# One-input steps of ranking and lists through PSUM, and a second last routing batch whose weights move behind the token splits, in a fused attention and expert kernel

## The chip, the cores and the metric

The kernel runs on one core of a Trainium2 chip. The metric is device time in microseconds (us) of one launch, as the median of three runs. A profile of one further execution gives the times of single instructions; all times in this document count from the start of that execution's span.

Engines are called by the names in the profile: PE (TensorE, matrix products), PEld (its weight loads), DVE (VectorE), ACT (ScalarE), POOL (GpSimd) and SP (SyncE, which issues DMAs). Each engine works through its own queue in order. SBUF is the memory that all engines share; PSUM holds the results of PE in banks of 128 x 512 fp32, and DVE and ACT can read and write it too.

## The reference

Causal attention with a decay bias over 8 batches, 8 heads, 576 positions and 64 columns a head; its output, 4608 tokens of 512 columns, is routed to one of 16 experts each (4 groups of 4), and each token's result is its expert's, scaled by two softmax weights:

```python
x = attn_out.transpose(0, 2, 1, 3).reshape(4608, 512)
g_logits = x @ w_group;  g_idx = np.argmax(g_logits, axis=1)
for g in range(4):
    xg = x[g_idx == g]
    e_logits = xg @ w_expert[g];  e_idx = np.argmax(e_logits, axis=1)
    for e in range(4):
        h = np.maximum(xg[e_idx == e] @ w1[g, e], 0.0)      # 512 -> 1024
        out[tokens] = (g_w * e_w)[:, None] * (h @ w2[g, e])  # 1024 -> 512
```

All data are fp32. The kernel gets the precision of an fp32 product from three products of rounded parts: high by high, low by high and high by low.

## The kernel before, in words

**Attention** handles 64 heads in 32 pairs, p = 0 to 31; a batch b is four pairs. For each head PE makes row maxima (`pm`), scores (`ps`) and the product with the values (`po`); the pair's output is normalised on DVE (`xT`, L352), split in a high part (`xTh`, on ACT) and a low part (`xTl`), turned on PE (`px`, L394) and written to `xs` in device memory. The order of this stage is written out by hand in strings of letters; `R` in them takes one step of the **router** (class `Router`), a generator for each batch.

**Routing a batch** (`Router.batch`): PE makes the logits (`lg`, `pl`, `pr`), turns them so that tokens lie on partitions (`plt`, L795); DVE finds the best group and expert of each token (L803 to L824, which ends with the one-hot `hot`); PE counts how many tokens each expert has (`pc`, L831); DVE gives each token a place in its expert's list (L848 to L873), and fills `val` with the parts of the token's number (L879). PE adds them to the lists (`listed(0, 2)`: `pi`, L886). `weights` makes the token's combined weight in three bf16 parts, L940 puts them in `val`, and `listed(2, 5)` (`pw`, L886) adds them to the lists as well.

**The transition** overlaps the last two routed batches (b = 6 and 7) with the start of the experts. `pick(0)`, run by the generator `first()` ahead of batch 6, chooses the first expert from the counts so far; `start()` in batch 6 lists its first 256 tokens, gathers their rows (`xg`, an indirect DMA on POOL's queue), and then runs `pick(1)` for the second expert, whose number `e` SP reads to load its weights (`raw`, L1015). The first expert is slot 0 with 256 tokens (class `Slot`: transposes `px` and splits `xh`, `xl` at L1069 to L1072, hidden layer `ph` L1131, output `py` L1186); the third group of 128 tokens of this expert comes from a list that is complete only after batch 7 (class `Tile`: `prr_x`, `xhr`, `xlr`, then products `pur`, L1273). Here the order of PE is the order of the code, and the other engines are put in order by a scheduler, with constraints: `after(...)` keeps what it encloses behind the instructions given, and `behind(tc, later, earlier)` keeps one instruction behind another.

**The weights of every expert** come as fp32 (`raw`) and are split in a high part on ACT (`wh`, L1017) and a low part on POOL (`wl`, L1020), or, for some pieces, on DVE (L1026, from a copy `pw` in PSUM).

**After batch 7** DVE takes the lists of all experts apart and ranks the experts by token count: `list_ids` (L617 to L619) makes token numbers of list entries and marks the empty ones, `order_key` and L1331 to L1337 rank the experts, `by_slot` (L1355) picks each slot's list. On DVE `xlr`, for which PE waits, comes behind most of these steps. Slots 1 to 15 then run one expert each, in the order of the ranks; this stage has an order of its own for PE, DVE and ACT, which the change leaves as it is.

Of the kernel before, what the change touches and what calls it, by code (L numbers as in the profile page):

```python
# [20 lines left out]
P = 128  # L21
# [3 lines left out]
E = 16  # L25
# [29 lines left out]
def attn_moe(ctx, tc, qk, v, s, wr, w1, w2, out, stop_at=None, dbg=None):  # L55
# [24 lines left out]
    st.listed = {}  # L80
    st.masks, st.av, st.gathered, st.lows = [], [], [], []
# [30 lines left out]
def attention(tc, qk, v, s, wr, xs, st):  # L112
# [3 lines left out]
    with ExitStack() as ctx:  # L116
# [138 lines left out]
        def scores(n, pt):  # L255
# [16 lines left out]
            def exps(u, ps, o):  # L272
                t, off, w = u[0]
                rows = KT[t][1]
                nc.scalar.activation(probs(pt, t, off)[:rows, 0:o], ps[:rows, :o], AF.Exp, scale=0.125)  # L275
                if u[0][1] == 0:
                    push("e", n, lambda: causal(u))
# [46 lines left out]
        def normalise(p, vals, sums):  # L324
# [31 lines left out]
            def high():  # L356
# [8 lines left out]
                st.xh = nc.scalar.copy(xh, x[:, 0:512])  # L365
                push("L", p, lambda: low(xh, xl, x))
# [16 lines left out]
        def route(b):  # L383
            if b == B - 2:
                rt[0].queue.append(rt[0].first())
            rt[0].queue.append(rt[0].batch(b, xtail.pop(b), *xhl.pop(b)))
# [235 lines left out]
def first_ids(nc, pool, st, c0, c1, want):  # L622

    V = nc.vector
    sh = [P, c1 - c0, E]
# [11 lines left out]
class Router:  # L637
# [72 lines left out]
    def logits(self, b, xh, xl, chunks):  # L710
# [9 lines left out]
        if chunks[-1] == 3:  # L720
            self.logged = b
            nc.tensor.matmul(ps[:52], self.wr_sb[:, 3], xh[:, 3], start=False, stop=True)
            return self.lg.pop(b)

    def pick(self, k):
# [6 lines left out]
        top = sm.tile([P, 1], F32, name=f"ktop{k}")  # L732
        V.tensor_reduce(out=top, in_=st.key, axis=AX.X, op=ALU.max)
        V.tensor_tensor(out=st.first[:, k], in0=st.key, in1=top.to_broadcast([P, E]), op=ALU.is_equal)
        t = sm.tile([P, E], F32, name=f"kt{k}")
# [8 lines left out]
    def start(self):  # L744

        nc, sm, st = self.tc.nc, self.sm, self.st
        V = nc.vector
        chosen = first_ids(nc, sm, st, 0, 2, ((0, 0, 2, st.ids0[:, 0:2]),))
# [5 lines left out]
        with after(self.tc, chosen):  # L754
            self.pick(1)
            t = sm.tile([P, E], F32, name="ku")
            V.tensor_scalar(out=t, in0=st.count, scalar1=-1.0, scalar2=256.0, op0=ALU.mult, op1=ALU.add)
            V.scalar_tensor_tensor(out=t, in0=t, scalar=0.0, in1=st.first[:, 0], op0=ALU.max, op1=ALU.mult)
            V.tensor_tensor(out=st.count, in0=st.count, in1=t, op=ALU.add)
        yield  # L760

    def batch(self, b, xtail, xh, xl):
# [9 lines left out]
        lT = self.lT  # L772

# [15 lines left out]
        nc.scalar.copy(xr, ps[:64, :])  # L789
        st.xrt = (nc.scalar if b == B - 1 else nc.sync).dma_start(self.xs[b * S + 512:(b + 1) * S], xr)  # L790
# [3 lines left out]
        for t in range(NB):  # L794
            nc.tensor.transpose(ps[:, t * 20:(t + 1) * 20], lT[:, t * P:(t + 1) * P], ident[:20, :20])  # L795
# [81 lines left out]
        C4 = [P, NB, E * NL]  # L877
        for j in range(2):
            (nc.gpsimd if b < B - 1 else V).tensor_tensor(  # L879
                out=val[:, j], in0=colf, in1=self.part[:, j, b].unsqueeze(2).to_broadcast(C4), op=ALU.mult)  # L880
# [14 lines left out]
        def weights(bank):  # L895
            nc.scalar.activation(ex, df, AF.Exp)
            yield 1
# [4 lines left out]
            V.tensor_reduce(out=wf, in_=ex, axis=AX.X, op=ALU.add)  # L902
# [18 lines left out]

        yield 2
        if b == B - 1:
            c3, c3p = yield from weights(self.ps_s(f"pk{b}"))
        pi = listed(0, 2, "pi")
        if b == B - 1:
            st.routed = first_ids(nc, sm, st, 0, 3, ((0, 2, 3, st.ids0[:, 2:3]), (1, 0, 3, st.ids1)))
        else:
            if b == B - 2:
                for _ in self.start():  # L930
                    yield
            c3, c3p = yield from weights(pi)
        for j in range(3):
            yield
            with after(tc, st.routed):
                if b < B - 1 and j == 0:
                    nc.gpsimd.tensor_tensor(out=val[:, 2 + j], in0=colf, in1=c3[:, j].unsqueeze(2).to_broadcast(C4),
                                            op=ALU.mult)
                else:
                    st.valued = V.tensor_tensor(out=val[:, 2 + j], in0=colf,  # L940
                                                in1=c3p[:, j].unsqueeze(2).to_broadcast(C4), op=ALU.mult)
        yield 2
        if b == B - 2:
            yield
        listed(2, 5, "pw")
# [5 lines left out]
def moe(tc, w1, w2, xs, st, out):  # L951
# [3 lines left out]
    with ExitStack() as ctx:  # L955
# [33 lines left out]
        class Expert:  # L989


            def __init__(self, u, e):
                self.u, self.e = u, e
                self.h, self.l, self.casts = [], [], []
# [650 lines left out]
```

## Time and profile before

| | us |
|---|---|
| median of 3 runs (lowest, highest) | 932.51 (931.83, 932.89) |
| profiled execution: time | 936.64 |
| its span, first to last instruction | 934.9 |
| PE busy in the span | 868.4 (93%) |
| DVE, ACT, POOL busy | 707.3, 629.3, 659.3 |

The time of a run is the span and what lies around it, 1.7 us in the profiled execution. Attention ends and slot 0 begins at about 447 us of the span, slot 1 begins at about 501 us. Busy time of PE is a sum over stretches with different limits: in most of the span PE is busy throughout, in the transition it isn't. The clock of PE that the profile gives is a share of full speed; 1.00 is 2.4 GHz, 0.50 is 1.2 GHz, and a value between the two is a mean over the stretch.

### The profile page before, as it was taken

Reading aid. Unit: us, or ns where it says so; the run is one execution under the profiler, and the core shown is the slowest. Engines: PE = TensorE matmul, PEld = TensorE weight load, DVE = VectorE, ACT = ScalarE, POOL = GpSimd, SP = SyncE. Lnnn points to the kernel's source line nnn. Section 1 sums busy time; section 2 is a strip of 40 time slices with the busy share of each in tenths; the row PEclk is TensorE's granted clock in tenths of the full one; section 3 lists DMA queues with packets and bytes.
Section 4 is the critical chain, followed back from the end, with each engine's and each line's share of the span. In section 5 each row is a group of like instructions: output and inputs, shape, how many; then the busy total and the mean of one; then the engine's idle time right before and its main releaser. Section 6 shows DMA issues by size and latency. Waiting matters only on the chain. (4 is left out here: it accounts for less than half of the span.)

```text
span 934.9 us, 17742 instructions
## 1 busy us (share of the span) xinstructions
PE 868.4 (93%) x5649; PEld 781.9 (84%) x5649; DVE 707.3 (76%) x1989; ACT 629.3 (67%) x1373; POOL 659.3 (71%) x762
## 2 busy tenths in 40 slices
PE   4899999999999999998968999999999999999993
PEld 3688787878878787887857999899999999999992
DVE  7676686858778686867577678898888898888830
ACT  3688786887878787867635466557676666766740
POOL 8898685877868686844764656666778778877750
PEclk9999999999999999999988999999999999999997
DMA  7776565565646655323534546455454556655510
GB/s 153 180 171 160 136 160 140 133 150 134 154 109 159 148 153 138 95 83 136 189 124 161 200 163 204 163 177 219 172 209 171 212 176 224 227 211 187 189 44 23
DMA packets 65005, 148.10 MB, mean 158 GB/s; under 512 B 7588, under 2 KB 40996, under 8 KB 54728
## 3 DMA queue, kind: packets, MB, share of 16 engines
q1 hardware_dynamic: 55020, 126.98, 46.1%
q0 software_dynamic: 7488, 18.89, 5.7%
q10 hardware_dynamic: 2396, 1.02, 0.4%
q8 instruction: 47, 0.77, 0.4%
q14 instruction: 54, 0.44, 0.2%
HBM read 108.97 MB, written 19.69 MB: 138 GB/s over the span
## 5 line engine op out<-in xcount | busy, mean ns | idle before, releaser
L1020 POOL TENSOR_TENSOR wl<-raw,wh 128x512 fp32r<-128x512 f32 x182 | 232.2, 1296 | 60.7 <-ACT wh L1017 42.7
L159 POOL TENSOR_TENSOR WB<-r,WA 64x576 fp32r<-64x576 f32 x128 | 180.9, 1413 | 23.9 <-ACT WA L156 7.6
L216 DVE CUSTOM_DVE_ANT_0 mx<-pm,mask 128x192 bf16<-128x192 f32 (+4 forms) x320 | 129.1, 419 | 39.5 <-PE pm L208 34.8
L1017 ACT CAST wh<-raw 128x512 fp32r<-128x512 f32 x256 | 154.0, 616 | 1.3 <-POOL wl L1020 0.7
L1131 PE MATMUL ph<-xl,wh 128*128 128x256 f32 (+13 forms) x512 | 145.5, 304 | 4.5 <-DVE xl L1092 4.5
L1131 PE MATMUL ph<-xh,wh 128*128 128x256 f32 (+13 forms) x512 | 144.2, 300 | 1.5 <-ACT xh L1091 1.4
L208 PE MATMUL pm<-WA 66*128 66x288 f32 (+4 forms) x384 | 126.0, 356 | 17.4 <-DMA WA<-ch 9.3
L265 PE MATMUL ps<-WA 68*128 68x320 f32 (+4 forms) x384 | 135.7, 357 | 6.8 <-ACT pu L275 3.7
L305 PE MATMUL po<-pt,VT 128*128 128x256 f32 (+3 forms) x512 | 122.0, 355 | 0.2 <-issue 0.2
L1186 PE MATMUL py<-hl,wh 128*128 128x256 f32 (+13 forms) x448 | 114.8, 304 | 5.0 <-DVE hl L1127 5.0
L1186 PE MATMUL py<-hh,wh 128*128 128x256 f32 (+13 forms) x448 | 113.8, 303 | 0.0
L267 PE MATMUL ps<-WB 128*128 128x320 f32 (+4 forms) x384 | 109.7, 299 | 0.0
L1232 DVE STREAM_TRANSPOSE yr<-yT 32x384 f32<-32x384 f32 (+1 forms) x208 | 104.5, 502 | 4.2
L305 PE MATMUL po<-pu,VT 128*128 128x320 f32 (+1 forms) x384 | 107.7, 389 | 0.0
L1087 DVE STREAM_TRANSPOSE xt<-xg 32x256 f32<-32x256 f32 (+1 forms) x208 | 102.5, 493 | 3.2
L1131 PEld LDWEIGHTS ph<-xl,wh 128*128 128x128 f32 x512 | 96.7, 189 | 7.9 <-DVE xl L1092 6.4
L1131 PEld LDWEIGHTS ph<-xh,wh 128*128 128x128 f32 x512 | 96.7, 189 | 3.4 <-ACT xh L1091 3.1
L305 PEld LDWEIGHTS po<-pt,VT 128*128 128x128 f32 x512 | 87.9, 193 | 12.8 <-issue 1.4
L208 PEld LDWEIGHTS pm<-WA 66*128 66x128 f32 (+1 forms) x384 | 68.7, 190 | 30.7 <-DVE mc L216 13.9
L1126 ACT ACTIVATE hh<-ph 128x256 fp32r<-128x256 f32 (+13 forms) x128 | 53.2, 420 | 59.6 <-PE ph L1131 59.2
L284 POOL TENSOR_SCALAR_AFFINE_SELECT pt<-pt 128x128 f32<-128x128 f32 (+2 forms) x192 | 63.9, 342 | 40.6 <-ACT pt L275 35.8
L1131 PE MATMUL ph<-xh,wl 128*128 128x256 f32 (+13 forms) x512 | 90.0, 299 | 0.0
(237 smaller groups left out, 1927.7 us busy)
## 6 DMA issues: line engine op xcount, KB each, us to landing
raw<-in_w_dram SPq DMA_DIRECT2D x64, 1024.0 KB
WB<-WA SPq DMA_DIRECT2D x64, 288.0 KB
r<-in_qk_dram SPq DMA_DIRECT2D x31, 576.0 KB
VT<-in_v_dram SPq DMA_DIRECT2D x32, 384.0 KB
xs<-xr SPq DMA_DIRECT2D x15, 512.0 KB
xs<-xrt SPq DMA_DIRECT2D x7, 128.0 KB
xg<-xs,ids POOLq DMA_INDIRECT x46, 4.8
out_dram<-yr,ids POOLq DMA_INDIRECT x43, 3.2
```

Of the source, the lines that this page charges most:

```text
L159: i = nc.gpsimd.tensor_tensor(out=wb[64 * a:64 * a + 64, a, h], in0=r[:, h, a], in1=w[0:64, a, h, QO:].bitcast(F32), op=ALU.subtract)
L208: nc.tensor.matmul(ps[:rows, :cw], WA[i][0:66, QA, h, QO + q0:QO + q0 + rows], WA[i][0:66, KA, h, QO + c0:QO + c0 + cw], start=True, stop= ...
L216: nc.vector.tensor_tensor_reduce(out=tmp[:rows, :cw], in0=ps[:rows, :cw], in1=mk[:rows], scale=1.0, scalar=-3.0e38 if c0 == 0 else mo, op0 ...
L265: nc.tensor.matmul(ps[:rows, o:o + w], WA[i][0:68, KA, h, QO + k0:QO + k0 + rows], WA[i][0:68, QA, h, QO + q0:QO + q0 + w], start=True, st ...
L267: nc.tensor.matmul(ps[:rows, o:o + w], WB[p % NBB][:, KA, h, k0:k0 + rows], WB[p % NBB][:, QA, h, q0:q0 + w], start=False, stop=True)
L305: i = nc.tensor.matmul(po[0][:, qa - base:qb - base], VT[p % NVT].rearrange("p t a d -> p (t a d)")[:, (3 * t + 1 + h) * 64:][:, 0:P], x[: ...
L1017: self.casts.append(nc.scalar.copy(h[:, j], raw[:, j]))
L1020: self.low = nc.gpsimd.tensor_tensor(out=l[:, j], in0=raw[:, j], in1=h[:, j].bitcast(F32), op=ALU.subtract)
L1087: V.transpose(dst[:, 0:n, :, j], src[:, 0:n, :, i])
L1131: self.products.append(nc.tensor.matmul(pss[f][:, :cap], w[f // 4][:, c, (f % 4) * P:(f % 4 + 1) * P], x[:, c, :cap], start=(c == 0 and w ...
L1186: self.products.append(nc.tensor.matmul(pss[c][:, :cap], w[2 + f // 4][:, f % 4, c * P:(c + 1) * P], x[:, f, :cap], start=(f == 0 and w is ...
L1232: V.transpose(dst[:, 0:n, :, i], src[:, 0:n, :, j])
```

## The change

**One-input steps.** `order_key`, `pick`, `first_ids` and the ranking after batch 7 get a PSUM bank for their intermediate results. A step that read SBUF and wrote SBUF with one tensor input (`TENSOR_SCALAR` in L609, L618 and L757, the copies to integers in L633, L1343 and L1381) now has its input or its output in PSUM. Steps with two tensor inputs mostly take one of them from PSUM, but not all: `key<-first,key`, `pk<-first,ie`, the comparison of all keys and `rank<-sel,ie` still read both from SBUF.

**The batch before the last (b = 6).** `pick(0)` becomes a step of the batch itself, which brings all its steps one `R` forward. Its `weights`, its three `val` steps and its `listed(2, 5)` no longer follow `start()`; they are kept (`self.rest`) and run in batch 7 after its `pr` copy; on DVE they lie behind the splits of slot 0. `pick(1)` (now `second()`) moves there too.

**The last batch (b = 7).** `listed(0, 2)` and the token numbers come ahead of `weights`; the token parts used in `val` come from PSUM.

**Order of PE.** The first products of slot 0 go through the columns of the hidden layer in another order, and `pc` and `pi` of batch 7 get other places among the products (`made[...]`). The six steps of `py` that go ahead of the third group stay.

The diff, cut to its core:

```diff
@@ order_key, first_ids @@
-def order_key(nc, st):
+def order_key(nc, st, key):
     V = nc.vector
-    V.tensor_scalar(out=st.key, in0=st.count, scalar1=16.0, scalar2=15.0, op0=ALU.mult, op1=ALU.add)
-    V.tensor_tensor(out=st.key, in0=st.key, in1=st.ie, op=ALU.subtract)
+    r = V.tensor_scalar(out=key, in0=st.count, scalar1=16.0, scalar2=15.0, op0=ALU.mult, op1=ALU.add)
+    V.tensor_tensor(out=st.key, in0=key, in1=st.ie, op=ALU.subtract)
+    return r
...
-    ids, emp = (pool.tile(sh, F32, name=f"{n}{c0}") for n in ("kids", "kemp"))
+    ids = pool.tile([P, c1 - c0, E], F32, name=f"kids{c0}{c1}")
+    emp = bank[:, 0:n].rearrange("p (c e) -> p c e", e=E)
...
-        idf = pool.tile([P, b - a], F32, name=f"kidf{k}{a}")
+        idf = bank[:, n + 4 * k:n + 4 * k + b - a]
@@ Router @@
-    def pick(self, k):
+    def pick(self, k, bank):
...
-        order_key(nc, st)
+        key, t, top = st.key, bank[:, E:2 * E], bank[:, 2 * E:2 * E + 1]
+        r = order_key(nc, st, bank[:, 0:E])
         if k:
-            V.scalar_tensor_tensor(out=st.key, in0=st.first[:, 0], scalar=-1.0e6, in1=st.key, op0=ALU.mult, op1=ALU.add)
+            V.scalar_tensor_tensor(out=key, in0=st.first[:, 0], scalar=-1.0e6, in1=key, op0=ALU.mult, op1=ALU.add)
...
-    def first(self):
-        self.pick(0)
-        yield
...
-        with after(self.tc, chosen):
-            self.pick(1)
-            t = sm.tile([P, E], F32, name="ku")
...
+    def second(self):
+        st, V = self.st, self.tc.nc.vector
+        bank = self.ps_s("pk6")
+        st.put_off.append(self.pick(1, bank))
+        t = bank[:, 3 * E:4 * E]
+        st.put_off.append(V.tensor_scalar(out=t, in0=st.count, scalar1=-1.0, scalar2=256.0, op0=ALU.mult, op1=ALU.add))
+        V.scalar_tensor_tensor(out=t, in0=t, scalar=0.0, in1=st.first[:, 0], op0=ALU.max, op1=ALU.mult)
+        V.tensor_tensor(out=st.count, in0=st.count, in1=t, op=ALU.add)
@@ batch @@
+        if b == B - 2:
+            self.pick(0, self.ps_s("pk5"))
+            yield
...
+        if b == B - 1:
+            self.second()
+            for _ in self.rest:
+                yield
         st.xrt = (nc.scalar if b == B - 1 else nc.sync).dma_start(self.xs[b * S + 512:(b + 1) * S], xr)
...
+        if b == B - 1:
+            bank = self.ps_s(f"pk{b}")
+            part = bank[:, 200:200 + 2 * NB].rearrange("p (j t) -> p j t", t=NB)
+            nc.scalar.copy(part, self.part[:, :, b])
...
         if b == B - 1:
-            c3, c3p = yield from weights(self.ps_s(f"pk{b}"))
+            listed(0, 2, "pi")
+            st.routed = first_ids(nc, sm, bank[:, 256:], st, 0, 3, ((0, 2, 3, st.ids0[:, 2:3]), (1, 0, 3, st.ids1)))
+            yield from finish(*(yield from weights(bank)))
+            return
         pi = listed(0, 2, "pi")
...
+        nc.scalar.activation(ex, df, AF.Exp)
+        yield from self.start(pi[:, 256:])
+        self.rest = rest()
@@ moe @@
-        for i, k in ((1, 3),):
-            behind(tc, st.gathered[i], st.masks[-k])
+        behind(tc, st.masks[-4], st.gathered[1])
...
+        bank = pt.tile([P, 512], F32, name="rank", tag="pt")
+        ie, key, t3 = st.ie, st.key, bank[:, 0:E * E].rearrange("p (a b) -> p a b", b=E)
...
+        list_ids(nc, st, idl, bank[:, 256:256 + NL * E].rearrange("p (c e) -> p c e", e=E), 0, NL)
+        order_key(nc, st, keyp)
...
-        list_ids(nc, st, idl, t4[:, 0], 0, NL)
...
-            behind(tc, st.av[-4], first.turned)
-            behind(tc, wts[0].casts[0], first.split[0])
-            behind(tc, wts[0].casts[2], st.evacs[-1])
+            behind(tc, first.turns[0], st.av[0])
+            behind(tc, st.av[2], first.turns[3])
+            for i in st.put_off:
+                behind(tc, i, first.split[1])
...
-            behind(tc, made[84], st.counted)
+            behind(tc, made[40], st.logged)
+            behind(tc, made[52], st.turned)
+            behind(tc, made[66], st.counted)
...
-            behind(tc, st.listed[0], made[39])
-            behind(tc, made[40], st.listed[0])
+            behind(tc, made[8], st.listed[0])
...
-            run(Y[6:7] + R[:1])
+            run(R[:1])
...
-            run(Y[7:] + R[1:5])
+            run(Y[6:] + R[1:5])
```

Where the work now stands. **PE, where the gathered rows of slot 0 are turned** (`px_0` to `px_3` read `xg`; `po` is the last product of attention, `px` from `xT` a pair's output, `pw` batch 6's weights in the lists). Before:

```order
L305 MATMUL po_0_6244<-pt_119,VT_116 128x256
L1069 MATMUL px_0_6573<-ident,xg_74 128x128
L305 MATMUL po_0_6244<-pu_120,VT_116 128x128
L1069 MATMUL px_0_6573<-ident,xg_74 128x128
L1069 MATMUL px_1_6578<-ident,xg_74 128x128 x2
L886 LDWEIGHTS rows_6098
L886 MATMUL pw_6250<-val_6109,rows_6098 128x192
```

And now:

```order
L305 MATMUL po_0_6210<-pt_119,VT_116 128x256
L305 MATMUL po_0_6210<-pu_120,VT_116 128x128
L305 MATMUL po_1_6216<-pt_119,VT_116 128x320
L393 MATMUL px_6218<-ident,xT_6163 128x128 x4
L305 MATMUL po_1_6216<-pt_119,VT_116 128x192
L1090 MATMUL px_0_6567<-ident,xg_74 128x128 x2
L1090 MATMUL px_1_6572<-ident,xg_74 128x128 x2
L305 MATMUL po_1_6216<-pt_119,VT_116 128x64
```

`px_0` and `px_1` moved behind more of attention's products, and `pw` of batch 6 is gone from here; it now follows `pr` of batch 7.

**DVE, from the turned logits of batch 7 to its one-hot** (`lmx` is the maximum of a token's logits, `hot` what PE's counts wait for; `pk` is the PSUM bank of `pick(1)`). Before:

```order
L803 TENSOR_REDUCE lmx_6339<-plt_6333 128x25
L805 TENSOR_TENSOR plt_6333<-plt_6333,lmx_6339 128x100
L808 TENSOR_TENSOR df_6342<-plt_6333,lmx_6339 128x100
L812 TENSOR_TENSOR eq_6344<-plt_6333,desc 128x100
L814 TENSOR_REDUCE plt_6333<-eq_6344 128x25
L816 TENSOR_TENSOR oh_6347<-plt_6333,desc 128x100
L822 TENSOR_TENSOR plt_6333<-plt_6333,desc 128x20
L824 TENSOR_TENSOR hot<-oh_6347,plt_6333 128x80
```

And now, from the last steps ahead of `lmx` on (six more follow, `hot` the last, three of them of `second()`):

```order
L903 TENSOR_TENSOR lists<-lists,pw_6320 128x192
L609 TENSOR_TENSOR key<-pk_6290,ie 128x16
L733 SCALAR_TENSOR_TENSOR key<-first,key 128x16
L734 TENSOR_REDUCE pk_6290<-key 128x1
L809 TENSOR_REDUCE lmx_6334<-plt_6328 128x25
L735 TENSOR_TENSOR first<-key,pk_6290 128x16
L811 TENSOR_TENSOR plt_6328<-plt_6328,lmx_6334 128x100
L736 TENSOR_TENSOR pk_6290<-first,ie 128x16
L814 TENSOR_TENSOR df_6337<-plt_6328,lmx_6334 128x100
L818 TENSOR_TENSOR eq_6339<-plt_6328,desc 128x100
L737 TENSOR_REDUCE pk_6290<-pk_6290 128x1
L820 TENSOR_REDUCE plt_6328<-eq_6339 128x25
```

`pick(1)` moved in among these steps; it stood ahead of the splits of slot 0, in batch 6. From `lmx` to `hot` there are 14 rows where there were 8.

**DVE, from the last list of batch 7 to `xlr`.** Before (the ranking stood ahead of these rows):

```order
L892 TENSOR_TENSOR lists<-lists,pw_6421 128x192
L618 TENSOR_SCALAR xts<-idl 128x64
L1340 TENSOR_TENSOR t_73<-sel,ie 128x256
L619 SCALAR_TENSOR_TENSOR idl<-idl,xts 128x64
L1341 TENSOR_REDUCE esl<-t_73 128x16
L1343 CAST esi<-esl 128x16
L1026 TENSOR_TENSOR wl_0_6875<-raw_0_6873,pw_0_0_6887 128x512
L1263 TENSOR_TENSOR xlr<-prr_x,xhr 128x4x128
```

And now (`rank` is the PSUM bank of the ranking):

```order
L903 TENSOR_TENSOR lists<-lists,pw_6414 128x192
L618 TENSOR_SCALAR rank<-idl 128x64
L619 SCALAR_TENSOR_TENSOR idl<-idl,rank 128x64
L608 TENSOR_SCALAR rank<-count 128x16
L609 TENSOR_TENSOR key<-rank,ie 128x16
L1359 SCALAR_TENSOR_TENSOR key<-first,key 128x16 x2
L1361 TENSOR_TENSOR rank<-key 128x256
L1047 TENSOR_TENSOR wl_0_6869<-raw_0_6867,pw_0_0_6881 128x512
L1362 TENSOR_REDUCE rank<-rank 128x16
L1285 TENSOR_TENSOR xlr<-prr_x,xhr 128x4x128
```

The ranking moved behind the list of `pw`, the empty marks go to PSUM, and the steps on `sel` that stood ahead of `xlr` moved behind it.

## Rows read from the trace of the kernel before

**Rows 1.** The page's first part: busy time, share of the span, instructions.

```profile
PE 868.4 (93%) x5649; PEld 781.9 (84%) x5649; DVE 707.3 (76%) x1989; ACT 629.3 (67%) x1373; POOL 659.3 (71%) x762
```

**Rows 2.** Windows: length, each engine's busy time (instructions), PE's clock, DMA share, GB/s.

```profile
440.00:450.00 10.00, 8.74 (x50) 7.51 (x51) 5.97 (x15) 7.01 (x17) 4.97 (x5) 0.83 0.30 87
...
470.00:480.00 10.00, 9.19 (x66) 8.98 (x67) 4.85 (x23) 2.45 (x6) 3.57 (x4) 0.83 0.36 123
...
490.00:500.00 10.00, 7.06 (x21) 5.66 (x22) 6.79 (x15) 0.60 (x1) 1.61 (x2) 0.62 0.61 225
...
540.00:560.00 20.00, 20.00 (x128) 20.00 (x127) 15.54 (x28) 11.16 (x23) 10.00 (x8) 1.00 0.43 162
```

**Rows 3.** Timeline of PE: start, length, instruction, count [idle before and its releaser].

```profile
439.99 0.55 PE L1069 MATMUL px<-ident,xg 128*128 128x128 f32 x3 [0.58 <-DMA xg<-xs,ids]
441.80 0.69 PE L886 MATMUL pw<-val,rows 128*128 128x192 bf16 x5 [1.26 <-DVE val L940]
...
451.49 2.08 PE L1131 MATMUL ph<-xh,wl 128*128 128x256 f32 x16
...
462.66 0.32 PE L831 MATMUL pc<-hot,ub 128*128 128x64 bf16 x2 [0.72 <-DVE hot L824]
...
467.47 0.38 PE L1186 MATMUL py<-hl,wh 128*128 128x256 f32 x1 [1.14 <-DVE hl L1127]
...
470.81 0.58 PE L1186 MATMUL py<-hl,wh 128*128 128x256 f32 x1 [2.50 <-DVE hl L1127]
...
483.79 0.50 PE L1273 MATMUL pur<-wh,xhr 128*128 128x512 f32 x1
492.94 0.80 PE L1273 MATMUL pur<-wh,xlr 128*128 128x512 f32 x1 [8.65 <-DVE xlr L1263]
...
500.46 0.80 PE L1069 MATMUL px<-ident,xg 128*128 128x128 f32 x6
```

**Rows 4.** Timeline of DVE from the ranking to `xlr`.

```profile
479.05 0.17 DVE L609 TENSOR_SCALAR key<-count 128x16 f32<-128x16 f32 x1
...
480.40 0.42 DVE L1335 TENSOR_REDUCE rank<-t 128x16 f32<-128x256 f32 x1
...
482.24 0.35 DVE L892 TENSOR_TENSOR lists<-lists,pw 128x192 f32<-128x192 f32 x1 [0.96 <-PE pw L886]
482.51 8.07 DVE L618 TENSOR_SCALAR xts<-idl 128x64 f32<-128x64 f32 x1
...
491.59 0.69 DVE L1026 TENSOR_TENSOR wl<-raw,pw 128x512 fp32r<-128x512 f32 x1
492.20 0.68 DVE L1263 TENSOR_TENSOR xlr<-prr_x,xhr 128x512 fp32r<-128x512 f32 x1
```

**Rows 5.** Timeline of POOL: the second expert's weight splits, with a memset between.

```profile
482.67 2.52 POOL L1020 TENSOR_TENSOR wl<-raw,wh 128x512 fp32r<-128x512 f32 x2
...
485.61 4.92 POOL L1020 TENSOR_TENSOR wl<-raw,wh 128x512 fp32r<-128x512 f32 x4
```

**Rows 6.** Timeline of DVE in batch 7, from the logits to `val`, and `val` later.

```profile
460.49 0.26 DVE L803 TENSOR_REDUCE lmx<-plt 128x25 f32<-128x100 f32 x1 [3.30 <-PE plt L795]
...
462.37 0.24 DVE L824 TENSOR_TENSOR hot<-oh,plt 128x80 bf16<-128x80 f32 x1
...
464.30 0.18 DVE L903 TENSOR_SCALAR pk<-pk 128x25 f32<-128x25 f32 x1
...
467.67 2.75 DVE L879 TENSOR_TENSOR val<-col,part 128x320 bf16<-128x320 bf16 x2
...
477.86 1.27 DVE L940 TENSOR_TENSOR val<-col,pk 128x320 bf16<-128x320 bf16 x3
```

**Rows 7.** Timeline of POOL: the first expert's last weight splits.

```profile
461.13 10.42 POOL L1020 TENSOR_TENSOR wl<-raw,wh 128x512 fp32r<-128x512 f32 x8 [2.28 <-ACT wh L1017]
```

**Rows 8.** Second expert: its number on DVE (timeline).

```profile
442.34 0.14 DVE L738 CAST e<-ktop 128x1 int32<-128x1 f32 x1
```

**Rows 9.** SP's instructions of L1015 from 458 to 462: durations in ns, starts.

```profile
L1015 SPq DMA_DIRECT2D raw<-in_w_dram x1: 337/337/337, 458.9 to 458.9; - x1
```

**Rows 10.** Timeline of ACT: the second expert's first casts.

```profile
471.17 2.17 ACT L1017 CAST wh<-raw 128x512 fp32r<-128x512 f32 x4
```

More of the change, by code (lines that the diff above doesn't have):

```diff
@@ L877, in batch @@
         C4 = [P, NB, E * NL]
+        part = self.part[:, :, b]
+        if b == B - 1:
+            bank = self.ps_s(f"pk{b}")
+            part = bank[:, 200:200 + 2 * NB].rearrange("p (j t) -> p j t", t=NB)
+            nc.scalar.copy(part, self.part[:, :, b])
         for j in range(2):
             (nc.gpsimd if b < B - 1 else V).tensor_tensor(
-                out=val[:, j], in0=colf, in1=self.part[:, j, b].unsqueeze(2).to_broadcast(C4), op=ALU.mult)
+                out=val[:, j], in0=colf, in1=part[:, j].unsqueeze(2).to_broadcast(C4), op=ALU.mult)
         EL = E * NL
@@ L901, in weights @@
             c3p = bank[:, 176:176 + 3 * NB].rearrange("p (j t) -> p j t", t=NB)
-            V.tensor_reduce(out=wf, in_=ex, axis=AX.X, op=ALU.add)
+            with after(tc, st.routed):
+                summed = V.tensor_reduce(out=wf, in_=ex, axis=AX.X, op=ALU.add)
+            if b == B - 2:
+                st.put_off.append(summed)
             V.tensor_scalar(out=wf, in0=wf, scalar1=1e-9, scalar2=None, op0=ALU.add)
@@ L920, in weights, with finish, rest @@
             return c3, c3p
+        def finish(c3, c3p):
+            for j in range(3):
+                yield
+                with after(tc, st.routed):
+                    if b < B - 1 and j == 0:
+                        nc.gpsimd.tensor_tensor(out=val[:, 2 + j], in0=colf, in1=c3[:, j].unsqueeze(2).to_broadcast(C4),
+                                                op=ALU.mult)
+                    else:
+                        st.valued = V.tensor_tensor(out=val[:, 2 + j], in0=colf,
+                                                    in1=c3p[:, j].unsqueeze(2).to_broadcast(C4), op=ALU.mult)
+            yield 2
+            listed(2, 5, "pw")
+        def rest():
+            yield from finish(*(yield from weights(pi)))
         yield 2
         if b == B - 1:
-            c3, c3p = yield from weights(self.ps_s(f"pk{b}"))
+            listed(0, 2, "pi")
+            st.routed = first_ids(nc, sm, bank[:, 256:], st, 0, 3, ((0, 2, 3, st.ids0[:, 2:3]), (1, 0, 3, st.ids1)))
+            yield from finish(*(yield from weights(bank)))
+            return
         pi = listed(0, 2, "pi")
[L926 to L945, printed above, removed]
+        if b < B - 2:
+            yield from rest()
+            return
+        nc.scalar.activation(ex, df, AF.Exp)
+        yield from self.start(pi[:, 256:])
+        self.rest = rest()
 NCH = 52
@@ L1118, in opening @@
                     for c in (0, 2):
-                        for f in (0, 3, 1, 2):
+                        for f in (1, 2, 0, 3):
                             half(f, c)
@@ L1327, in moe @@
         S3 = [P, E, E]
-        ie, key, t3 = st.ie, st.key, st.t3
-        order_key(nc, st)
+        bank = pt.tile([P, 512], F32, name="rank", tag="pt")
+        ie, key, t3 = st.ie, st.key, bank[:, 0:E * E].rearrange("p (a b) -> p a b", b=E)
+        keyp, rank, eslp = (bank[:, 320 + i * E:320 + (i + 1) * E] for i in range(3))
+        idp = bank[:, 384:384 + NL * E].rearrange("p (e c) -> p e c", c=NL)
+        esl = mc.tile([P, E], F32, name="esl")
+        idl = mc.tile([P, NL, E], F32, name="idl")
+        list_ids(nc, st, idl, bank[:, 256:256 + NL * E].rearrange("p (c e) -> p c e", e=E), 0, NL)
+        order_key(nc, st, keyp)
         for k in range(2):
@@ L1364, in moe @@
             run(X)
-            behind(tc, st.av[-4], first.turned)
-            behind(tc, wts[0].casts[0], first.split[0])
-            behind(tc, wts[0].casts[2], st.evacs[-1])
+            behind(tc, first.turns[0], st.av[0])
+            behind(tc, st.av[2], first.turns[3])
+            for i in st.put_off:
+                behind(tc, i, first.split[1])
+            for i in range(4):
+                behind(tc, wts[0].casts[i], first.highs[1 if i < 2 else 3])
+            behind(tc, first.highs[2], st.evacs[-1])
+            behind(tc, wts[0].lows[14], rest.last)
             h = first.h_items()
```

72 lines of the change are left out of this document (33 added, 39 removed).

## The prediction

> **What bounds the kernel now.** I read the page first: PE is busy for 93% of the span [rows 1], so I looked for the stretches in which it isn't. The windows show them: from 540 us on, a stretch is full (20.00 of 20.00 at clock 1.00), while in the transition PE is idle for microseconds and its clock is 0.83, 0.83 and 0.62 in three windows of 10 us [rows 2]. What ends that idle time stands in brackets on PE's timeline [rows 3]: 0.58 (a gather) and 1.26 (batch 6's `val`), 0.72 (`hot`), 1.14 and 2.50 (`hl`, late on DVE), 8.65 (`xlr`). Together 14.9 us. The clock adds to it: 0.83 over 10 us means 3.4 us at 1.2 GHz, in which 1.7 us of full-speed work are lost; each of these slow stretches follows waits of PE.
>
> The cause of the longest wait stands on DVE's timeline [rows 4]: one `TENSOR_SCALAR` on 64 elements (L618, SBUF to SBUF) lasts 8.07 us, and `xlr` is queued behind it. POOL's splits of weights ran from 482.67 to 490.53 without a pause [rows 5], and L618 ended with them, at 490.58. A second kind of delay is milder: L879, with two inputs in SBUF, took 2.75 us for two steps inside POOL's run of eight splits (10.42 us, so 1.3 each) [rows 6, 7]; the like step with one input in PSUM (L940) takes 1.27 for three, 0.42 each [rows 6]. So a two-input step lost 2.75/2 - 0.42 = 0.95 us, about a split's remainder, and was let in between two splits: its two steps ended at 470.42, the run at 471.55. A step from PSUM to PSUM (L903, 0.18 us at 464.30) lost nothing in the same run.
>
> The Trainium skill, "SBUF — State Buffer", section "Who interferes with whom", says that VectorE's copies and `tensor_scalar` in a two-port mode, and its instructions with two SBUF inputs, share a port pair with GpSimd, and that the loser is blocked for a whole instruction of the other. For L879 the trace agrees (0.95 us); for L618 it doesn't, which was held through six splits and a memset. By the rule alone L618 would have lost one split at most, and moving it would be worth 1.3 us; by the row it is worth 8, and the sum below goes by the row.
>
> **The change, part by part.** PE does the same products, so the sum is what its waits and its slow stretches become.
>
> *Gathers and `pw` of batch 6.* `px_0` now stands behind more of attention's products, the token numbers are no longer interleaved with `weights` on DVE, and `pw` has left the place where PE waited 1.26. Both waits go (1.84), and with them the reason for the slow stretch from 440 to 450 (1.7). Term: **-3.5**. Bounds: 0 if other waits take their place, -3.5.
>
> *Batch 6's steps one `R` earlier.* Costed at nothing: attention's products lie around each of them on PE, only in another order; a bank that isn't free would cost a few tenths.
>
> *Less cover.* PE begins slot 0 about 4 us earlier, while ACT still evacuates attention's last products and casts weights between the splits of `xh`, and the last pair's `xT` reads two SBUF inputs beside POOL's first splits (up to one split, 1.3). I take two small waits, **+1.0** (bounds 0 and 2).
>
> *`pick(1)` among the steps to `hot`.* Before, eight steps took 460.49 to 462.61 [rows 6]. Now 14 stand there; half of them are independent of their neighbour, so I take 0.2 us each, 2.8. Ahead of `lmx` now stand the list of `pw`, L609, L733 and L734, some 0.9 (0.35 for the list [rows 4], the rest as L609's 0.17). L733 and L736 read two SBUF inputs in a run of splits: 2 x 0.95 = 1.9. PE has 14 products between `plt` and `pc`, at 2.08/16 = 0.13 [rows 3] 1.8 us. The wait becomes 2.8 + 0.9 + 1.9 - 1.8 = 3.8 in place of 0.72: **+3.1**. Bounds: +1.2 without any delay by POOL, +3.8 with a full split each. Behind it the clock falls, as it did behind the wait of 2.50 (1.7); the small products of `pc` take part of it: **+1.4** (bounds 0, 1.7). Queued behind on DVE is `df`, hence ACT's exponential and, behind that, the first expert's last casts; POOL splits the rest in the meantime, and PE needs them only 100 products later.
>
> *Expert number.* It was ready at 442.34 [rows 8], SP issued the load at 458.9, when a buffer came free [rows 9], and ACT cast at 471.17 [rows 10]. Now the number comes at about 459, and SP must read it first; the load starts some 2 to 3 us later. Costed at nothing, since the casts still stand behind slot 0's `hh` and the weights of batch 7, 10 us on; without that cover it would cost those 3 us.
>
> *Token parts through PSUM.* `val` takes 0.85 instead of 2.75, so `hl` is no longer behind it, and `pi` stands after 8 products of `py` where its data are there. The waits 1.14 and 2.50 go, and the slow stretch behind them (1.7): **-5.3**. Bound: -1.9, `val`'s own saving.
>
> *Ranking and `xlr`.* L618 goes to PSUM: no 8 us. In the new order everything from the list to `xlr` runs behind `pw`: the list 0.35, L618 and L619 0.4, the ranking 1.77 (479.05 to 480.82, without POOL in the way), L1026's like 0.6, `xlr` 0.68 [rows 4], 3.8 in all. Three of these steps have two SBUF inputs, beside the second expert's splits: 3 x 0.95 = 2.85. PE meanwhile has `prr_x`, 16 products (2.08) and one of 0.50 [rows 3], about 3.0. The wait becomes 3.8 + 2.85 - 3.0 = 3.65 in place of 8.65: **-5.0**. Bounds: a wait of 0.8 (-7.9) and of 4.7 (-4.0, a full split each). The slow clock behind this wait (0.62 in 490 to 500 [rows 2]) I leave as it is; if it doesn't fall, up to 2 more.
>
> **Sum:** -3.5 + 1.0 + 3.1 + 1.4 - 5.3 - 5.0 = **-8.3 us**. It is made against the profiled execution: a span of 934.9 and 936.64 in all. Its median of runs is 4.1 lower, at 932.51; I take the difference over: 932.5 - 8.3 = **924.2**. Behind the transition PE is full [rows 2], so what is gained there reaches the end.
>
> **The rivals.**
> *The two-input steps meet no split.* POOL has gathers and a memset between its splits, and if DVE comes then, 1.9 and 2.85 fall away, and perhaps the slow clock: 8.3 + 4.75 = 13 to 15 us less, about **918.5**. Against it: POOL's runs are long and one step after the other would have to be lucky.
> *PSUM on one side doesn't free a one-input step.* No row has a step from SBUF to PSUM beside a split; L903 had PSUM on both sides. Then L618 waits out the six splits, of which some 6 us are left when it comes, and the ranking behind it runs freely: a wait of 3.8 + 6 - 3.0 = 6.8, the last term is -1.8, the sum -5.1, **927.4**.
> *Slower: two-input steps wait out POOL's whole run, as L618 did.* Place: L733 ahead of `hot`, with some 7 us of splits left until ACT's casts run out behind the exponential, so 6 more than I take; and the first ranking step, with all six splits ahead of it (7.8), 5 more. Sum -8.3 + 11 = +2.7, **935**. It decides from 8.3/5 = 1.7 us more than 0.95 for each of the five steps, that is from two splits each. Against it: L879 was let in twice inside one run [rows 6, 7].
> *The stalls only move.* If the first term comes to nothing and each bound is the worse one, the sum is near 0: the same.
>
> **How the numbers follow.** Forecast 0.55, no meeting 0.2, one side not enough 0.1, the slower rival 0.08, the same 0.07. The first three are faster; a change within 0.2% (1.9 us) is about what a measurement of this kernel can't tell from none. So faster 0.85, the same 0.07, slower 0.08. The range for 8 in 10 runs from 917, near the first rival, to 929, beyond the second: the forecast alone would be 921 to 927.
>
> **What would show it.** Right: no DVE step of over 2 us between 470 and 490; `val` below 0.9 for two; PE waiting for `hot` some 4 us and for `xlr` some 4 us, and no wait ahead of `pw`; the first `px` of slot 1 at about 492 instead of 500.46. Wrong, to the better: L733, L736 and the ranking's comparison at their own length. Wrong, to the worse: one of them, or L618, as long as several splits; or a wait of ACT for the second expert's load.

## The result, and the profile after

The changed kernel takes **923.94 us** (median of 6 runs, 922.53 to 926.30); the kernel before, run beside it, takes 934.47 (median of 6, 931.83 to 938.75). The ratio is 0.9886, with a 95% interval of 0.9856 to 0.9916: faster by 1.1%. Between the two profiled executions the span falls from 934.9 to 922.4 us, and slot 1 begins at 488.03 instead of 500.46 [rows 3], so the difference lies ahead of slot 1. Not all of it lies in the transition. Attention's last score product, the same place in both orders (2491 products stand ahead of it), starts 2.15 us earlier; before, then now:

```profile
436.73 0.28 PE L267 MATMUL ps<-WB 128*128 128x192 f32 x1
434.58 0.28 PE L267 MATMUL ps<-WB 128*128 128x192 f32 x1
```

Within attention PE's clock fell to 1.2 GHz twice in the profile of before (0.98 in the windows from 100 to 200 and from 200 to 300 us) and once in this one (0.98 from 300 to 400). The first fall before came at about 156 us behind waits of 0.28 and 0.37 us at L208; the same waits stand at the same place in this profile, with no fall behind them. In further profiles of the same two kernels (experiments 9 and 10) it fell at other places, so I don't count these 2.15 us for the change. They were there when attention's last batch began (its first `ps` at 389.94 before and 387.72 now); up to there PE, DVE, ACT and POOL run the same instructions in the same order in both. From the last `ps` to slot 1 the profile shows 63.73 us before and 53.45 now: the transition is 10.3 us shorter.

Page of the changed kernel, its first part, as in [rows 1]:

```profile
PE 862.9 (94%) x5649; PEld 778.1 (84%) x5649; DVE 706.4 (77%) x1990; ACT 628.8 (68%) x1374; POOL 659.6 (72%) x762
```

PE does the same 5649 instructions in 5.5 us less, so part of the difference is clock. The windows, as in [rows 2]:

```profile
440.00:450.00 10.00, 9.62 (x72) 7.97 (x70) 6.78 (x21) 7.67 (x19) 7.78 (x7) 1.00 0.77 261
...
470.00:480.00 10.00, 4.27 (x34) 3.59 (x33) 8.04 (x9) 5.08 (x12) 8.93 (x8) 0.87 0.33 134
480.00:490.00 10.00, 8.66 (x39) 7.08 (x40) 7.37 (x18) 2.38 (x6) 1.08 (x1) 0.79 0.64 226
490.00:500.00 10.00, 9.72 (x59) 8.86 (x59) 8.56 (x14) 9.29 (x20) 8.55 (x8) 1.00 0.42 117
```

In the transition one slow stretch is left, in and behind the one long wait that is left. PE's timeline, as in [rows 3]:

```profile
437.64 0.78 PE L305 MATMUL po<-pt,VT 128*128 128x320 f32 x2 [0.49 <-POOL xTl L370]
443.18 0.39 PE L1153 MATMUL ph<-xh,wh 128*128 128x256 f32 x1 [0.38 <-DVE xl L1093]
453.09 0.48 PE L801 MATMUL plt<-ident,lT 20*128 20x20 f32 x5 [0.20 <-DVE lists L903]
456.22 0.32 PE L837 MATMUL pc<-hot,ub 128*128 128x64 bf16 x2 [0.78 <-DVE hot L830]
...
472.16 0.66 PE L1282 MATMUL prr_x<-ident,xg 128*128 128x128 f32 x4 [0.69 <-DVE lists L903]
...
481.29 0.80 PE L1295 MATMUL pur<-wh,xlr 128*128 128x512 f32 x1 [6.32 <-DVE xlr L1285]
...
488.03 0.80 PE L1090 MATMUL px<-ident,xg 128*128 128x128 f32 x6
```

The waits for the gather, for batch 6's `val` and for `hl` are gone; `hot` costs 0.78 as before (0.72); `xlr` costs 6.32 instead of 8.65. DVE's timeline, as in [rows 4, 6], says why:

```profile
453.16 0.33 DVE L733 SCALAR_TENSOR_TENSOR key<-first,key 128x16 f32<-128x16 f32 x1
...
454.09 0.65 DVE L736 TENSOR_TENSOR pk<-first,ie 128x16 f32<-128x16 f32 x1
...
460.36 0.88 DVE L890 TENSOR_TENSOR val<-col,pk 128x320 bf16<-128x320 bf16 x2
...
471.75 0.35 DVE L903 TENSOR_TENSOR lists<-lists,pw 128x192 f32<-128x192 f32 x1 [2.25 <-PE pw L897]
472.02 0.22 DVE L618 TENSOR_SCALAR rank<-idl 128x64 f32<-128x64 f32 x1
...
472.95 6.29 DVE L1359 SCALAR_TENSOR_TENSOR key<-first,key 128x16 f32<-128x16 f32 x2
...
480.55 0.68 DVE L1285 TENSOR_TENSOR xlr<-prr_x,xhr 128x512 fp32r<-128x512 f32 x1
```

And POOL's splits beside them, as in [rows 5, 7]:

```profile
450.94 12.49 POOL L1040 TENSOR_TENSOR wl<-raw,wh 128x512 fp32r<-128x512 f32 x10
...
471.58 7.42 POOL L1040 TENSOR_TENSOR wl<-raw,wh 128x512 fp32r<-128x512 f32 x6
```

L618, 8.07 us before, is 0.22 now that it writes to PSUM, beside the same splits. Behind it the ranking's first step L1359, which reads both its inputs from SBUF, lasts 6.08 us (the second 0.17) and ends at 479.03, with POOL's run at 479.00. The stall has passed from a one-input step to the next two-input step.

### The profile page after: what moved, and what is told of

It is laid out like the page before. It is cut to its first block, busy times and chain, and to the rows that moved or that the text cites. A ratio compares the mean times of both kernels' runs of the same rounds, so it can differ in the third digit from the quotient of the medians.

```text
span 922.4 us, 17746 instructions
## 1 busy us (share of the span) xinstructions
PE 862.9 (94%) x5649; PEld 778.1 (84%) x5649; DVE 706.4 (77%) x1990; ACT 628.8 (68%) x1374; POOL 659.6 (72%) x762
## 5 line engine op out<-in xcount | busy, mean ns | idle before, releaser
L208 PE MATMUL pm<-WA 66*128 66x288 f32 (+4 forms) x384 | 125.2, 354 | 17.3 <-DMA WA<-ch 9.4
L208 PEld LDWEIGHTS pm<-WA 66*128 66x128 f32 (+1 forms) x384 | 68.5, 190 | 30.6 <-DVE mc L216 13.5
```

The source lines that it names most:

```text
L208: nc.tensor.matmul(ps[:rows, :cw], WA[i][0:66, QA, h, QO + q0:QO + q0 + rows], WA[i][0:66, KA, h, QO + c0:QO + c0 + cw], start=True, stop= ...
```

## The experiments

Times are medians; each ratio is to the kernel before, run on the same chip, with its 95% interval. Spans are of the profiled execution. Where attention's clock would blur a comparison, I count from its last `ps` product, as above; attention is the same in all these runs.

**1. Keys in PSUM.** The ranking's keys stay in the bank; one copy brings them to SBUF for the comparison, whose other input is PSUM.

```diff
-    order_key(nc, st, keyp)
+    order_key(nc, st, keyp, keyp)
...
-        V.scalar_tensor_tensor(out=key, in0=st.first[:, k], ..., in1=key, ...)
-    V.tensor_tensor(out=t3, in0=bc(key, 1, S3), in1=bc(key, 2, S3), op=ALU.is_gt)
+        V.scalar_tensor_tensor(out=keyp, in0=st.first[:, k], ..., in1=keyp, ...)
+    V.tensor_copy(key, keyp)
+    V.tensor_tensor(out=t3, in0=bc(keyp, 1, S3), in1=bc(key, 2, S3), op=ALU.is_gt)
```

> The ranking's keys stay in PSUM, so that its two steps L1359, held 6.08 us in the changed kernel, take one input from SBUF and one from PSUM. Theory (a step with two SBUF inputs waits out POOL's run of splits, one input in PSUM frees it): both at 0.2 us, no step of DVE above 1.3 us from the list at 471.8 to xlr, xlr done at about 475.7, PE's wait for it 0.7 in place of 6.3, 5.6 us less. Given back at most 2 to 3 if the next step with two SBUF inputs (t3 from sel and ie, behind xlr) is held instead and slot 1's xl behind it comes late. So 917 to 921 against 923.9. Rival 1 (the run holds whatever DVE does at that place, PSUM or not): the step stays at about 6 us and the time within 1 of 923.9. Rival 2 (what follows, slot 1's gathers and the second expert's splits, comes no earlier): the wait for xlr shrinks, but PE waits as long ahead of slot 1's products, within 1.5 of 923.9.

Measured: 919.14 us (916.84 to 922.78), ratio 0.9828 (0.9802 to 0.9855), span 918.7. DVE's timeline:

```profile
474.29 0.39 DVE L1359 SCALAR_TENSOR_TENSOR rank<-first,rank 128x16 f32<-128x16 f32 x2
...
477.81 3.16 DVE L1367 TENSOR_TENSOR rank<-sel,ie 128x256 f32<-128x256 bf16 x1
```

and PE's:

```profile
476.57 0.50 PE L1295 MATMUL pur<-wh,xlr 128*128 128x512 f32 x1 [0.28 <-DVE xlr L1285]
...
484.30 0.54 PE L1090 MATMUL px<-ident,xg 128*128 128x128 f32 x3 [1.12 <-DVE ids L1412]
```

Both steps are at 0.2 us and the wait of 6.32 is 0.28: two inputs from SBUF were the cause of this hold. The hold falls on the next such step (L1367), and part of the gain goes into waits of 1.12, 0.73 and 0.28 ahead of slot 1's products.

**2. The same with L618 from SBUF to SBUF.**

```diff
-    list_ids(nc, st, idl, bank[:, 256:256 + NL * E]..., 0, NL)
+    emps = mc.tile([P, NL, E], F32, name="emps")
+    list_ids(nc, st, idl, emps, 0, NL)
...
```

> The run before this one, with the one-input step L618 writing to SBUF again, as in the kernel before the change. Theory (a step from SBUF to SBUF waits out what is left of POOL's run, as in the kernel before, 8.07 us): L618 lasts 6 to 7 us, to the run's end at about 479, PE's wait for xlr is back at 6 to 7 us, 923 to 925. Rival (one split at most, as the page's rule has it): L618 lasts up to 1.3 us, PE's wait is up to 2 us, 918 to 922.

Measured: 919.48 us, ratio 0.9829 (0.9801 to 0.9856). Inconclusive: without the bank to wait for, L618 was scheduled before POOL's run, at 471.22 beside a gather, and took 0.24 us. In this kernel L1367's step (its line is L1368 here) was held 4.21 us.

**3. L618 forced behind the list of `pw`.** `st.added` is the last sum that `listed()` makes, that of `pw`.

```diff
+                st.added = V.tensor_tensor(out=dst, in0=dst, ...)
...
+    with after(tc, st.added):
+        list_ids(nc, st, idl, emps, 0, NL)
```

> In the run with the step L618 back in SBUF it was put ahead of POOL's run and met no split. Here the same kernel (keys in PSUM, L618 from SBUF to SBUF) has L617 and L618 behind the list of pw, so that L618 comes inside the run of six splits, as in the kernel before. Theory (a step from SBUF to SBUF is held to the run's end): L618 lasts 6 to 7 us, PE waits 6 to 7 us for xlr instead of 0.3, 4 to 6 us more than with the keys in PSUM alone (919.1). Rival (one split at most): L618 1.3 us or less, PE's wait 0.5 to 1.8, within 2 us of 919.1.

Measured: 929.38 us, ratio 0.9936 (0.9912 to 0.9959). The step ahead of L618, L617, was moved with it, has two SBUF inputs and took the hold itself; L618 came behind the run, at 0.19. DVE's and PE's timelines:

```profile
476.29 7.36 DVE L617 SCALAR_TENSOR_TENSOR idl<-lists 128x64 f32<-128x64 f32 x1
```

```profile
487.15 0.79 PE L1295 MATMUL pur<-wh,xlr 128*128 128x512 f32 x1 [7.92 <-DVE xlr L1285]
```

So neither expectation was tested on L618; what it does show is the price of one held step ahead of `xlr`: 10 us between the medians of 1 and 3, on two sets of runs. Of the 9.5 us between the two profiled spans 2.9 lie in attention, which the edit leaves alone (the last `ps` is at 436.20 in 1 and at 439.13 here), so some 6.6 us belong to the step. That a one-input step is held rests on the kernel before alone ([rows 4], and 6.79 us in its second profile, below).

**4. `xlr` ahead of the ranking.** `st.ranked` is the first step of L1359, `rest.split[1]` is `xlr`.

```diff
+            st.ranked = i if k == 0 else st.ranked
...
+            behind(tc, st.ranked, rest.split[1])
```

> The changed kernel with xlr put ahead of the ranking's steps on DVE; nothing else moves but what stands behind them. Theory: xlr is done at 474.2, PE waits for it 0.3 us or less in place of 6.3; the first L1359 is held as before, now from 474.2 to 479, and the ranking, the token numbers and slot 1's xl behind it come as late as in the changed kernel, so PE, which is at slot 1 some 6 us earlier, waits 3 to 4 us for xl: 2 to 3 us less in all, 921 to 922. Rival (the ranking's lateness costs PE nothing): 6 us less, 917 to 918. Rival (held steps depend on what was issued ahead of them, not on POOL): L1359 at 0.2 us.

Measured: 921.27 us, ratio 0.9859 (0.9832 to 0.9886), span 918.7. DVE, then PE:

```profile
471.77 5.47 DVE L1359 SCALAR_TENSOR_TENSOR key<-first,key 128x16 f32<-128x16 f32 x2
```

```profile
483.11 0.87 PE L1090 MATMUL px<-ident,xg 128*128 128x128 f32 x3 [4.19 <-DVE ids L1413]
```

No wait for `xlr`, the same hold, and 4.19 us of it return at slot 1's first `px`, which needs the ranking's bank: the token numbers (`ids`) are read out of it last. The wait was expected ahead of `xl`, not there. From the last `ps` to slot 1 it is 45.2 us instead of 53.4, and from slot 1 to the end 441.0 instead of 434.4: moving the victim returned 6.6 of the 8.2 us.

**5. Batch 6's weights ahead of the token splits**, as before the change; the rest as changed.

```diff
-            if b == B - 2:
-                st.put_off.append(summed)
...
-        self.rest = rest()
+        yield from rest()
+        self.rest = ()
```

> The changed kernel with the weights of batch 6 ahead of the token splits again: its products pw stand ahead of slot 0's transposes on PE, as in the kernel before. Theory (term of -3.5): PE waits some 1.3 us ahead of pw or 0.6 ahead of the transposes and the clock falls behind it, 440 to 450 at 0.8 to 0.9 instead of 1.00: 1.3 to 3.5 us more, 925.2 to 927.4. Rival (moving the transposes behind more of attention's products removed both waits by itself): within 1 of 923.9.

Measured: 928.87 us (923.03 to 931.67), ratio 0.9928 (0.9898 to 0.9959), span 928.7. PE's timeline and the window behind it:

```profile
439.88 0.68 PE L897 MATMUL pw<-val,rows 128*128 128x192 bf16 x5 [2.42 <-DVE val L943]
```

```profile
440.00:450.00 10.00, 9.62 (x54) 7.82 (x53) 3.28 (x8) 6.84 (x16) 3.57 (x4) 0.83 0.37 113
```

The wait ahead of `pw` and the clock of 0.83 are back; the wait for the gather (0.58 before) isn't. The move is worth 4.9 us by the medians (3.9 by the ratios, 0.0042 of 934.47) and 4.8 from the last `ps` to slot 1 (58.2 us for 53.4), a little more than the term of 3.5, since `val` is later than before the change (2.42 for 1.26).

**6. `val` of batch 7 from SBUF.**

```diff
             nc.scalar.copy(part, self.part[:, :, b])
+            part = self.part[:, :, b]
```

> The changed kernel with the token parts of batch 7 read from SBUF again by L890's two steps (the copy to PSUM stays, unread). Theory (term of -5.3, of which -1.9 is val's own): val takes 2.75 in place of 0.88, hl behind it comes 1.9 late, PE waits 1 to 2 us for it and the clock falls behind that: 1.9 to 3.6 us more, 925.8 to 927.5. Rival (the new order on PE, with pi behind 8 products of py, covers val whatever it takes): val 2.75 or less, no wait of PE above 0.5 there, within 1 of 923.9. Rival (a run in which DVE is not let in): val is held to the run's end, 3 us.

Measured: 924.16 us (922.95 to 924.54), ratio 0.9891 (0.9874 to 0.9908). DVE, then PE:

```profile
459.33 2.39 DVE L891 TENSOR_TENSOR val<-col,part 128x320 bf16<-128x320 bf16 x2
```

```profile
461.78 0.56 PE L898 MATMUL pi<-val,rows 128*128 128x128 bf16 x5 [1.10 <-DVE val L891]
```

The two steps lose 1.51 us, PE waits 1.10 for them, and the clock stays at 1.00 there. In this execution the ranking's first step happened to be let in after 2.12 us, and the wait for `xlr` was 4.46. The total can't tell the 1.10 from none: from the last `ps` to slot 1 it is 54.1 us, and 53.4, 54.1 and 53.2 in the three profiles of the changed kernel (below). So by PE's wait PSUM brings about 1.1 of the 5.3 us. The rest, by subtraction, comes with the other parts of the change, the order of PE's products first of all; no run takes that order alone.

**7 and 8. Gathers, or memsets, ahead of the first expert's run of ten.** Three gathers of POOL, of rows that are overwritten later; as a control, three memsets in their place.

```diff
+        for t in range(3):
+            more = gather(nc, xs, xgs[1], ...)          # 8: nc.gpsimd.memset(xgs[1], 0.0)
+            for i in range(5, 8):
+                behind(tc, wts[0].lows[i], more)
```

> A probe of where a step with two SBUF inputs is let in between two splits of POOL and where it is held to the run's end. In all kernels so far the runs that held it (L618 and L1359) stood right behind gathers of POOL, and those that let it in (L733, L736, val) did not. Here three more gathers of POOL, with rows that are overwritten later, stand right ahead of the run of ten splits of the first expert. Theory (a run behind gathers holds): L617's kids step or L736, whichever comes inside the run, lasts until the run's end, several us, where it took 0.65 and 1.06 without these gathers. Rival (gathers have no part in it): no such step above 1.3 us. The time tells nothing: POOL's run is 3.9 us later by itself, so up to 4 us more.

> The control to the run with three more gathers: three memsets of the same tile (1.38 us each) stand in their place, so that POOL's run of ten splits starts as late, and L617's kids step meets it with the same four or five splits to go. Theory (gathers ahead of a run make it hold DVE): with memsets in their place L617 is let in at the next boundary, 1.3 us or less, where it lasted 5.26 behind gathers. Rival (what matters is where in the run, or that several splits are still to come, not the gathers): L617 lasts 3 us or more here too.

Measured: 927.63 and 925.22 us, one run each. L617's step on DVE, with gathers and with memsets:

```profile
461.10 5.26 DVE L617 SCALAR_TENSOR_TENSOR kids<-lists 128x48 f32<-128x48 f32 x1
```

```profile
462.43 0.82 DVE L617 SCALAR_TENSOR_TENSOR kids<-lists 128x48 f32<-128x48 f32 x1
```

and POOL's run beside it, in the same order:

```profile
453.73 12.52 POOL L1040 TENSOR_TENSOR wl<-raw,wh 128x512 fp32r<-128x512 f32 x10
```

```profile
455.64 12.52 POOL L1040 TENSOR_TENSOR wl<-raw,wh 128x512 fp32r<-128x512 f32 x10
```

Behind gathers L617 was held to the run's end (466.25); behind memsets it ended at 463.25, just after a split did (463.16), with four splits still to come, as many as there were behind the gathers. This speaks for the gathers, but it is one pair, and the steps also arrive at other moments of a split (0.11 and 0.69 us before the next one began).

**9 and 10. The two kernels profiled again**, unchanged: the changed kernel twice, the kernel before once.

> The changed kernel once more, for a second profile. With the token parts from SBUF the same ranking step, in the same run of POOL, was let in after 2.12 us where it had been held 6.08, though nothing near it was changed. Theory A (the program's order decides where a step is let in): L1359 is held to the end of the run of six splits again, 6 us, PE's wait for xlr 6 to 6.5. Theory B (it is decided anew in each execution): another length, some number of splits, 1 to 6 us, and PE's wait shorter by the difference. Time 922 to 926 by both.

> As the run before it, a third profile of the changed kernel. Theory A: L1359 6 us in all three. Theory B: the three differ by a split or more (1.24 us).

> The kernel before the change, for a second profile. Theory A: L618 8 us, held to the run's end, and val (L879) let in at two boundaries, 2.75 us, as in the first. Theory B: at least one of them by a split or more different.

Measured: 925.02 us (ratio 0.9905, 0.9880 to 0.9930), 925.05, and 936.24 for the kernel before. The second profile repeats the first (6.19 for the two steps, wait 6.22). DVE and PE in the third:

```profile
474.23 3.52 DVE L1359 SCALAR_TENSOR_TENSOR key<-first,key 128x16 f32<-128x16 f32 x2
```

```profile
480.80 0.80 PE L1295 MATMUL pur<-wh,xlr 128*128 128x512 f32 x1 [4.57 <-DVE xlr L1285]
```

The same program, another length: how long such a step is held is decided in the execution. Of the eight profiles in which L1359 reads both inputs from SBUF, six held it to the run's end and two (this one and experiment 6) let it in earlier, after 2.30 and 2.12 us. The shorter wait brought next to nothing here: the 23 products from its end to slot 1 took 8.14 us (480.80 to 488.94) instead of 6.74, since PE's clock stayed at 1.2 GHz to 486.7 instead of 484.2. From the last `ps` to slot 1 the three profiles of the changed kernel show 53.4, 54.1 and 53.2 us, the two of the kernel before 63.7 and 64.4; the ten us between them agree with the 10.5 between the medians. The kernel before repeated itself: L618 6.79 us to the run's end, `val` 2.77.

**11. All of the ranking through PSUM.** Experiment 1, with the expert index and the list of token numbers in the bank too.

```diff
+    V.tensor_copy(iep, ie)
...
-    V.tensor_tensor(out=t3, in0=sel, in1=bc(ie, 1, S3), op=ALU.mult)
+    V.tensor_tensor(out=t3, in0=sel, in1=bc(iep, 1, S3), op=ALU.mult)
-            by_slot(idp, idl, 0, E)
+            by_slot(idp, idlp, 0, E)
```

> The run with the keys in PSUM, and with the two next steps freed too: the ranking's second comparison reads the expert index from a copy in PSUM (there it was held 3.16 us) and the token numbers by slot read their list from PSUM. Theory: no step of DVE above 1.3 us from 471 to 490, the token numbers ready 2 to 3 us earlier, so the waits of PE ahead of slot 1's products (1.12, 0.73 and 0.28) go: 1 to 2 us less than 919.1, 917 to 918. Rival (these waits are replaced by others, slot 1's gathers or the second expert's splits): within 0.7 of 919.1.

Measured: **917.44 us** (914.83 to 919.05), ratio **0.9811** (0.9791 to 0.9832), span 915.6: the lowest median of all. The interval overlaps that of experiment 1; from the last `ps` to the end the profiles show 480.2 us here and 482.5 there. No step of DVE from 471 to 490 lasts over 1.3 us. The windows:

```profile
470.00:480.00 10.00, 9.51 (x60) 8.10 (x60) 7.60 (x23) 6.47 (x14) 9.64 (x9) 1.00 0.69 255
480.00:490.00 10.00, 9.41 (x62) 8.39 (x62) 8.72 (x17) 8.85 (x19) 6.47 (x7) 1.00 0.68 215
```

PE is nearly full at clock 1.00, where the changed kernel has 0.87 and 0.79; there is no wait for `xlr`, and 0.54 is the longest ahead of slot 1's products.

## Why the prediction came out

The predicted time, 924.2 us, is 0.3 from the median, and that is luck: two errors of about 2 us met in it. The base was the median of three runs, 932.5; the six runs beside the changed kernel, 931.83 to 938.75, gave 934.47. From there the change brought 10.5 us, not the 8.3 of the sum. Of the signs that the prediction names, `val` below 0.9 and no wait ahead of `pw` came. A step of DVE over 2 us between 470 and 490 came too, against the forecast (6.08), PE waited 0.78 and 6.32 for `hot` and `xlr`, not some 4 each, and slot 1 began at 488.03, not at 492.

Term by term, from the waits and windows of before and after:

- **Gathers and `pw`, -3.5: right.** Both waits are gone and the window from 440 to 450 is at 1.00; experiment 5 brings the wait ahead of `pw` and the slow clock back.
- **Batch 6's steps one `R` earlier, 0: right.** From the first to the last `ps` of attention's last batch it is 46.79 us before and 46.86 now.
- **Less cover, +1.0: right.** Two waits of 0.49 and 0.38.
- **`pick(1)` ahead of `hot`, +3.1 and +1.4: mis-sized; it measured +0.3 (0.06 at `hot`, 0.20 ahead of `plt`), with no fall of the clock.** The forecast wait was 3.8 us. Of the 2.8 that it had too much, 1.4 is the price of a two-input step: L733 and L736 lost 0.16 and 0.48 (they take 0.17 each in experiment 7, where they met no split), not 0.95 each, and only L736 stands behind `lmx`. Another 0.7 is cover: of the 0.9 of steps ahead of `lmx` all but 0.20 ran while PE still had work ahead of `plt`. The last 0.7 is length: from `lmx` at 453.61 to the end of `hot` at 456.17 the fourteen steps took 2.56 with L736's delay, 2.1 without (forecast 2.8). The 0.95 came from `val`, each of whose steps met a split some 0.3 us after it had begun; L733 and L736 met theirs later and ended with them (453.48 and 454.75, the splits at 453.45 and 454.70). The Trainium skill, "SBUF — State Buffer", section "Who interferes with whom", has the engine that comes first hold the shared pair for its whole instruction while the other is blocked. At these two steps the trace agrees.
- **Expert number, 0: right.** The first casts of the second expert stand at 467.94, ahead of 471.17 before [rows 10], and PE waits for none of them.
- **Token parts, -5.3: right in sum (-5.1).** The waits of 1.14 and 2.50 and the slow stretch behind them are gone. That stretch had cost 1.5, not 1.7: the clock fell at 470.3, and PE was idle until 470.81. Experiment 6 divides the sum: about 1.1 is PSUM, the rest by subtraction the other parts, the order of PE above all.
- **Ranking and `xlr`, -5.0: mis-sized.** The wait fell by 2.3, not 5.0, and 0.69 ahead of `prr_x` came on top. The failed step is again 0.95 for a two-input step, on the other side: L1359 was held to the run's end, 5.9 us beyond its own 0.17. This is the mechanism of the third rival at one of its two places. The same page of the Trainium skill has the other engine blocked for a whole instruction. Here the step waited for the end of five splits. The slow clock behind the wait, which the forecast left as it was, changed by no more than the profiles differ: the 23 products from the wait's end to slot 1 took 7.52 us before (492.94 to 500.46) and 6.74 now, and 6.79, 7.41 and 8.14 in the profiles taken again. The clock of a whole window (0.62 and 0.79) says less, since PE was idle in much of the slow stretch.

The measured terms are -3.5 + 0.9 + 0.3 - 5.1 - 2.3 + 0.7 - 0.8 = -9.8, of 10.3 between the last `ps` and slot 1. The other 2.1 of the 12.5 between the spans lie in attention, ahead of the first instruction that the change moves. So the forecast was right on what moves and, on both sides, wrong on what a two-input step costs beside POOL: 1.4 too dear at `hot`, with 1.4 of clock behind it that did not fall, and 2.7 too cheap at the ranking. "PSUM on one side doesn't free a one-input step" fell: L618 at 0.22 beside the splits.

What stays open is what decides whether such a step is let in between two splits. In ten profiles L733 and L736 met the run of ten with no gathers ahead of it, and were let in at the next boundary each time (0.67 us at most), but these are nearly the same two arrivals ten times over. In the run of six behind the gathers the first two-input step was refused at one boundary or more in all eleven profiles that had one. The moment of arrival alone doesn't decide: L733 came 0.26 us before the next split began and was let in, L1367 in experiment 1 came 0.32 before and was not.

## What to carry to other kernels

While POOL works through a run of instructions on SBUF, a DVE step with two SBUF inputs can cost anything between the rest of one instruction (0.16 us here) and what is left of the whole run (up to 7.36). Where a result is waited for, price it by the run, and look for the next such step in the queue: freeing one hands the hold to the one behind it, until all that lie ahead of a waited-for result read one input from PSUM. A price taken at one point of a split doesn't hold at another. A shorter wait isn't all gained where PE's clock is still low behind it. And the base of a prediction made from three runs can be off by as much as a term; a landmark ahead of the change, as the last `ps` here, takes out what differs before it.

## What the runs showed of the hardware that was not expected

A two-input step of 16 elements lasted 6.08, 5.98 and 2.30 us at the same place in three executions of one program. When `val` (320 elements) is let in, POOL pays: the split that starts beside it in experiment 6 lasts 1.52 us instead of 1.29; behind the small L733 and L736 the splits keep their length (1.28 and 1.27). And one operand is enough to end the hold: with one input in PSUM the same step took 0.18 us beside the same splits.
